# Query and key transposes of two batches moved from TensorE to the DMA crossbar, in a kernel of windowed attention and a SwiGLU block

## The chip, the cores and the metric

The kernel runs on one core of one Trainium2 chip. The metric is the device time of one execution in microseconds (us). The kernel before was run three times: 268.59, 268.65 and 269.51 us, median 268.65. A profiled execution is longer than its span (first to last instruction) by what lies around it.

## The reference

Attention over 4 batches of 8 heads, 768 positions and 64 elements a head, in which a query sees the 8 first keys ("global") and the 96 last ones up to its own ("local"), with a bias that falls with the distance by a slope of its head; its result, 3072 tokens of 512 elements, goes through a SwiGLU block with 1536 inner elements.

```python
scores = scale * np.matmul(q, k.transpose(0, 1, 3, 2))
is_global = pos[None, :] < n_global
is_local = (rel >= 0) & (rel < n_local)            # rel = query - key
scores = np.where(is_global | is_local, scores + bias, -1e9)
a = softmax(scores)                                # over the keys
x = np.matmul(a, v)  ->  [B * S, H * D]
g = x @ w_gate
out = (g * sigmoid(g) * (x @ w_val)) @ w_out
```

Inputs and output are fp32; the kernel computes in fp16 with fp32 sums.

## The kernel before

**Attention.** The unit of work is a pair of heads (`Pair(b, hp)`, four pairs in each batch), as two heads of 64 elements fill 128 partitions. Keys are cut into 7 chunks of 120, and each chunk is stored as 128 columns of `kT`, the 8 global keys first (columns 0 to 7), then its 120 own. So a query window of 216 meets its global and its local keys in one matmul. `transposes` (L186) makes `qT` and `kT` of a pair: 24 TensorE transposes of 128x64 blocks (L193) from the staged rows `qst` and `kst` into PSUM, then ScalarE copies them out: `qT` (L198) and `kT` in two pieces (L204, on VectorE for batch 0), then a VectorE copy spreads the 8 global keys over the 7 chunks (L208). `qst` and `kst` have two buffers each; their rows hold 6 positions of a head side by side, so that each piece of a load is 768 bytes in SBUF. `scores` (L212) multiplies a third of the chunks ("bank" 0, 1 or 2), takes the exponential on ScalarE (L227) and multiplies with the mask on VectorE or GpSimd (L234 for bank 1, L238 for the others). `values` (L240) sums denominators (`den`) and numerators (`num`) for half of the positions; VectorE inverts (L269, L270) and spreads (L275) the denominators, ScalarE copies `num` to `ns` (L290), and GpSimd multiplies into `xT` (L279).

**Feed-forward.** Tokens go in 8 blocks `t` of 384, two to a batch. For each block and each of 12 slices `f` of 128 inner elements there is a group of 4 gate matmuls and one of 4 value matmuls (L307), a tanh on ScalarE (L318), two VectorE products (L320, L324), and from block 1 on a quarter of an output tile of the block before, 3 matmuls (L334). Gate and value products share three PSUM banks. Every fourth quarter completes an output tile, which ScalarE copies to `osb` (two buffers, L339) and SyncE stores (L341).

**What sets the order.** The order of each engine's work is written out by hand. The loop at the end goes through the feed-forward groups; each group earns a share `work * quota` of an attention step, and each time a whole step is owed the next one in `plan` is emitted. `plan` gives each run of blocks a list of steps: `first(b)` has transposes, scores and values of the first half of batch `b`, `second(b)` the second half, and `both(b)` mixes the second half of batch `b` with the first half of `b + 1`: 13 steps, over blocks 2 and 3 for batch 2 and blocks 4 and 5 for batch 3, though a list starts as soon as the one before is used up.

Loads are issued by GpSimd (they cast fp32 to fp16), through the table `loads`, whose index is 12 `t` + `f`:

```python
    def both(b):
        x, y = second(b), first(b + 1)
        return x[:3] + [y[0], x[3]] + y[1:]
...
    for b, base, step in ((2, 15, 1), (3, 32, 2)):
        loads[base] = [lambda b=b: (stage(b), load_qk(b, 0, 4))]
        loads[base + step] = [lambda b=b: load_qk(b, 4, 8)]
        for c in range(NCH):
            loads[base + step * (2 + c)] = [lambda b=b, c=c: load_v_rest(b, c)]
```

SyncE's queue carries, after the start, the output stores alone. GpSimd's carries loads, mask products and `xT` products in one order.

Of the kernel before, what the change touches and what calls it, by code (L numbers as in the profile page):

```python
# [10 lines left out]
FP16 = mybir.dt.float16  # L11
# [4 lines left out]
KC = 120  # L16
# [21 lines left out]
def kernel(  # L38
# [12 lines left out]
    nc = tc.nc  # L51

    B, H, S, D = q.shape
    NG, NL = int(n_global), int(n_local)
    assert (B, H, S, D) == (4, 8, 768, 64)
    assert (NG, NL) == (8, 96)
    NP = H // 2
# [6 lines left out]
    NCH = 7  # L64
# [16 lines left out]
    sb = ctx.enter_context(tc.tile_pool(name="sb", bufs=1))  # L81
    sb2 = ctx.enter_context(tc.tile_pool(name="sb2", bufs=2))
    sb3 = ctx.enter_context(tc.tile_pool(name="sb3", bufs=3))
    ps = ctx.enter_context(tc.tile_pool(name="ps", bufs=1, space=bass.MemoryType.PSUM))

    ctx.enter_context(tc.manual_schedule())
# [10 lines left out]
    kTs = [sb.tile([128, NCH * 128], FP16, name=f"kT{i}") for i in range(NP)]  # L97
# [8 lines left out]
    def stage(b):  # L106
        qst[b] = sb2.tile([128, H, J * D], FP16, name="qst", tag="qst")
        kst[b] = sb2.tile([128, H, J * D], FP16, name="kst", tag="kst")

    def load_qk(b, h0, h1):  # L110
        for st, src in ((qst[b], q), (kst[b], k)):
            nc.gpsimd.dma_start(  # L112
                out=st[:, h0:h1, :],
                in_=src[b, h0:h1].rearrange("h (p j) d -> p h (j d)", p=128))
# [6 lines left out]
    def load_v_rest(b, c):  # L121
        n = min(KC, S - KC * c)
        nc.gpsimd.dma_start(  # L123
            out=vSs[b][NG:NG + n, c, :, :],
            in_=v[b, :, KC * c:KC * c + n, :].rearrange("h p d -> p h d"))
# [4 lines left out]
    def load_globals():  # L130
        nc.gpsimd.dma_start(
            out=vG.rearrange("p b h d -> p (b h) d"),
            in_=v[:, :, 0:NG, :].rearrange("b h p d -> p (b h) d"))
        for b in range(B):
            nc.sync.dma_start(
                out=vSs[b][0:NG, :, :, :],
                in_=vG[:, b, :, :].unsqueeze(1).broadcast_to([NG, NCH, H, D]))

    wg = sb.tile([128, NC, DFF], FP16, name="wg")
    wv = sb.tile([128, NC, DFF], FP16, name="wv")  # L140
# [22 lines left out]
    def bank(name, dt=FP32, cols=512):  # L163
        tags = state["tags"]
        tag = tags[state["n"] % len(tags)]
        state["n"] += 1
        return ps.tile([128, cols], dt, name=name, tag=tag)
# [13 lines left out]
    class Pair:  # L181
# [4 lines left out]
        def transposes(self):  # L186
            b, hp = self.b, self.hp
            trq = bank("trq", FP16, S)
            trk = bank("trk", FP16, S)
            for st, tr in ((qst[b], trq), (kst[b], trk)):  # L190
                for j in range(J):
                    for hi in range(2):
                        nc.tensor.transpose(  # L193
                            tr[64 * hi:64 * hi + 64, 128 * j:128 * j + 128],
                            st[:, 2 * hp + hi, D * j:D * j + D], ident)
            self.qT = sb2.tile([128, S], FP16, name="qT", tag="qT", bufs=NP)
            self.kT = kTs[hp]
            nc.scalar.copy(  # L198
                out=self.qT.rearrange("r (p j) -> r p j", j=J),
                in_=trq.rearrange("r (j p) -> r p j", j=J))  # L200
            k3 = self.kT.rearrange("r (c m) -> r c m", m=128)
            t3 = trk.rearrange("r (j p) -> r p j", j=J)
            for c0, c1, n in ((0, 6, KC), (6, 7, S - 6 * KC)):
                (nc.vector.tensor_copy if b == 0 else nc.scalar.copy)(  # L204
                    out=k3[:, c0:c1, NG:NG + n].rearrange("r c (p j) -> r c p j", j=J),
                    in_=t3[:, 20 * c0:20 * c0 + (c1 - c0) * (n // J), :].rearrange(
                        "r (c p) j -> r c p j", c=c1 - c0))
            nc.vector.tensor_copy(  # L208
                out=k3[:, :, 0:NG],
                in_=k3[:, 0, NG:2 * NG].unsqueeze(1).broadcast_to([128, NCH, NG]))  # L210

        def scores(self, bk, mul_eng):  # L212
            hp = self.hp
            sc = [bank("scA"), bank("scB")]
            for c in range(NCH):
                cb, col, q0, n = chunks[c]
                if cb != bk:
                    continue
                for hi in range(2):
                    r = slice(64 * hi, 64 * hi + 64)  # L220
                    nc.tensor.matmul(  # L221
                        sc[hi][:, col:col + n],
                        lhsT=self.kT[r, 128 * c:128 * c + 128],
                        rhs=self.qT[r, q0:q0 + n], start=True, stop=True)
            for hi in range(2):
                at = sb2.tile([128, BANK], FP16, name="at", tag=f"at{hi}{bk}", bufs=NP)
                nc.scalar.activation(out=at, in_=sc[hi][:, 0:BANK], func=AF.Exp, scale=scale)  # L227
                self.at[hi, bk] = at
            for hi in range(2):
                at = self.at[hi, bk]  # L230
                m = masks[:, 2 * hp + hi, :]
                if bk == 1:
                    a2 = at.rearrange("p (c w) -> p c w", c=2)
                    mul_eng.tensor_mul(  # L234
                        a2, a2, m[:, WIN:2 * WIN].unsqueeze(1).broadcast_to([128, 2, WIN]))
                else:
                    o = WIN // 2 * bk
                    mul_eng.tensor_mul(at, at, m[:, o:o + BANK])  # L238
# [111 lines left out]
    stage(1)  # L350
    load_qk(0, 0, 2)
    load_globals()
    load_v(0, 0)
    load_v(0, 1)
# [16 lines left out]
    pairs = {(b, hp): Pair(b, hp) for b in range(B) for hp in range(NP)}  # L371
# [15 lines left out]
    for t in range(4 + 2 * (NP - 1)):  # L387
# [3 lines left out]
        for hp in range(NP):  # L391
            s = t - 2 * hp
# [17 lines left out]
    def sc(b, hp, bk):  # L410
        on_vector = b == 0 or bk == 0 or (bk == 2 and hp % 2 == 0)
        return lambda: pairs[b, hp].scores(bk, nc.vector if on_vector else nc.gpsimd)

    def va(b, hp, half):
        return lambda: pairs[b, hp].values(half, b == 0)

    def tr(b, hp):
        return pairs[b, hp].transposes

    def second(b):  # L420
        return [[sc(b, 0, 2), sc(b, 1, 2)], [sc(b, 2, 2), sc(b, 3, 2)],
                [va(b, 0, 1), va(b, 1, 1)], [va(b, 2, 1), va(b, 3, 1)]]

    def first(b):
        return [[tr(b, 0), tr(b, 1)],
                [sc(b, 0, 0), sc(b, 0, 1)], [sc(b, 1, 0), sc(b, 1, 1)],
                [va(b, 0, 0), tr(b, 2)], [sc(b, 2, 0), sc(b, 2, 1)],
                [va(b, 1, 0), tr(b, 3)], [sc(b, 3, 0), sc(b, 3, 1)],
                [va(b, 2, 0)], [va(b, 3, 0)]]

    def both(b):
        x, y = second(b), first(b + 1)
        return x[:3] + [y[0], x[3]] + y[1:]


    single = [[sc(0, 0, 2)], [sc(0, 1, 2)], [va(0, 0, 1)], [sc(0, 2, 2)],
              [va(0, 1, 1)], [tr(1, 0)], [sc(0, 3, 2)], [va(0, 2, 1)], [va(0, 3, 1)], [tr(1, 1)]]
    plan = [((0,), single), ((1,), first(1)[1:]), ((2, 3), both(1)),
            ((4, 5), both(2)), ((6,), second(3))]

    loads = {10: [lambda: load_qk(1, 4, 8)]}
    for c in range(4, NCH):
        loads[8 + c] = [lambda c=c: load_v_rest(1, c)]
    for b, base, step in ((2, 15, 1), (3, 32, 2)):
        loads[base] = [lambda b=b: (stage(b), load_qk(b, 0, 4))]
        loads[base + step] = [lambda b=b: load_qk(b, 4, 8)]
        for c in range(NCH):
            loads[base + step * (2 + c)] = [lambda b=b, c=c: load_v_rest(b, c)]


    NT = TOK // TB
# [79 lines left out]
```

The softmax here doesn't subtract the row's maximum and nothing guards it: scores larger than these inputs give would overflow.

## Time and profile before

| what | value |
|---|---|
| median of three runs | 268.65 us |
| the profiled execution: its time | 268.58 us |
| the profiled execution: its span | 266.7 us |
| mean granted TensorE clock | 0.986 |
| 192 + 192 transposes on TensorE, mean of one | 239 and 243 ns |
| copies of `qT` on ScalarE, 16 | 12.9 us busy |
| copies of `kT` on ScalarE, 12 + 12 | 9.3 + 2.8 us busy |
| loads of `qst` and `kst` of batches 2 and 3 | 384 KB each, four to a batch |
| output stores on SyncE | 24, 256 KB, 2.0 us to landing |

In the profile a line such as `L193` is a line of the kernel, PE is TensorE, DVE VectorE, ACT ScalarE, POOL GpSimd and SP SyncE; `trq<-ident,qst` says what an instruction writes and reads. A row of 40 digits gives the busy share of an engine in tenths for 40 equal slices of the span. The chain is followed back from the last instruction, at each step to what released it. In a timeline, each row has a start, a length and, in brackets, the idle time before it with its releaser; the DMA-issuing instructions of GpSimd appear as `DMA_DIRECT2D`. Tokens of block 1 are under way on TensorE from about 54 to 86 us, those of block 2 to about 118, of block 3 to about 149.

### The profile page before, as it was taken

What the parts mean: (1) busy time and instruction counts of PE and PEld (TensorE: products, weight loads), DVE (VectorE), ACT (ScalarE), POOL (GpSimd) and SP (SyncE); (2) the same over time, 40 slices, a digit from 0 to 9 for tenths busy, and PEclk for the clock granted to TensorE, in tenths of its full rate; (3) what the DMA queues carried; (4) which work ended last, traced back from release to release, by engine and by line L of the source; (5) the groups of instructions that cost most, each with busy time, mean ns of one, the idle gap of its engine ahead of it and who ended that gap; (6) DMA issues with size and microseconds to landing.
All of it is one profiled execution on the core that took longest, in us unless ns stands there. A gap on an engine that the chain in (4) does not pass through costs nothing.

```text
span 266.7 us, 5704 instructions
## 1 busy us (share of the span) xinstructions
PE 247.8 (93%) x2240; PEld 142.0 (53%) x2240; DVE 174.8 (66%) x389; ACT 140.9 (53%) x297; POOL 112.1 (42%) x130
## 2 busy tenths in 40 slices
PE   1668899899999999999999999999999999999993
PEld 0444456456556555555556555565566555555541
DVE  2488799786877576557767485766778655555610
ACT  3657745678466656755464656573572333332321
POOL 8985562268987226365565152414342200000000
PEclk9995999999999999999999999999999999999999
DMA  8999999955996100967545200100110111001122
GB/s 103 168 167 195 193 205 206 177 57 34 209 176 42 47 39 2 157 91 101 65 60 37 49 19 24 39 28 15 42 39 2 39 42 41 21 18 42 39 79 79
DMA packets 45529, 21.27 MB, mean 80 GB/s; under 512 B 28256, under 2 KB 42432, under 8 KB 45504
## 3 DMA queue, kind: packets, MB, share of 16 engines
q0 software_dynamic: 41504, 14.20, 46.8%
q1 hardware_dynamic: 4000, 6.72, 6.9%
q8 instruction: 17, 0.28, 0.4%
q14 instruction: 8, 0.07, 0.1%
HBM read 28.58 MB, written 6.29 MB: 131 GB/s over the span
## 4 chain that ended last, share of the span: by engine, by line
PE 74%; DMA 12%; POOL 5%; ACT 5%; issue 2%; DVE 1%; ACTq 0%; POOLq 0%
PE ops L334 23%; PE vps L307 21%; PE gps L307 19%; DMA kst<-in_k_dram 8%; DMA wv<-in_moe_w_val_dram 4%; PE den L256 3%; PE num L256 3%; PE scA L221 3%; ACT at L227 2%; POOL vS L117 1%; PE trq L193 1%; POOL qst L112 1%; PE trk L193 1%; ACT kT L204 1%; ACT osb L339 1%
## 5 line engine op out<-in xcount | busy, mean ns | idle before, releaser
L318 ACT ACTIVATE th<-gps 128x384 f32<-128x384 f32 x96 | 47.9, 499 | 65.2 <-PE gps L307 64.2
L320 DVE SCALAR_TENSOR_TENSOR sl<-th,gps 128x384 f32<-128x384 f32 x96 | 52.6, 548 | 42.9 <-ACT th L318 42.3
L307 PE MATMUL gps<-xT,wg 128*128 128x384 f16 x384 | 79.1, 327 | 0.8 <-DVE xT L282 0.5
L307 PE MATMUL vps<-xT,wv 128*128 128x384 f16 x384 | 79.1, 327 | 0.7 <-DVE sl L320 0.7
L334 PE MATMUL ops<-wo,hT 128*128 128x512 f16 x288 | 76.0, 379 | 0.6 <-ACT osb L339 0.6
L324 DVE TENSOR_TENSOR hT<-vps,sl 128x384 f16<-128x384 f32 x96 | 52.7, 549 | 8.7 <-PE vps L307 1.1
L307 PEld LDWEIGHTS <-wg 128*128 128x128 f16 x384 | 36.1, 98 | 32.9 <-issue 1.9
L307 PEld LDWEIGHTS <-wv 128*128 128x128 f16 x384 | 36.2, 98 | 26.9 <-issue 4.0
L279 POOL TENSOR_TENSOR xT<-ns,rb 128x384 f16<-128x384 f32 x24 | 23.9, 997 | 59.4 <-DVE rb L275 52.3
L334 PEld LDWEIGHTS <-hT 128*128 128x128 f16 x288 | 27.1, 98 | 25.4 <-issue 1.2
L227 ACT ACTIVATE at<-scA 128x432 f16<-128x432 f32 x48 | 25.8, 537 | 16.6 <-PE scB L221 16.6
L234 POOL TENSOR_TENSOR at<-at,masks 128x432 f16<-128x432 f16 x24 | 23.7, 1010 | 15.7 <-ACT at L227 10.3
L227 ACT ACTIVATE at<-scB 128x432 f16<-128x432 f32 x48 | 26.1, 543 | 0.0
L339 ACT ACTIVATE osb<-ops 128x512 f32<-128x512 f32 x24 | 14.4, 602 | 18.7 <-PE ops L334 18.5
L123 POOL DMA_DIRECT2D vS<-in_v_dram x24 | 21.6, 901 | 3.9 <-DMA wo<-in_moe_w_out_dram 1.6
L238 DVE TENSOR_TENSOR at<-at,masks 128x432 f16<-128x432 f16 x52 | 20.4, 413 | 3.8 <-ACT at L227 3.3
L256 PE MATMUL den<-at,ones 128*64 128x216 f16 (+6 forms) x288 | 17.8, 238 | 1.8 <-DVE at L234 1.3
L290 ACT COPY ns<-num 128x384 f32<-128x384 f32 x24 | 11.5, 478 | 14.3 <-PE num L256 12.1
L275 DVE STREAM_TRANSPOSE rb<-dR 128x384 f32<-128x384 f32 x32 | 18.3, 572 | 1.0
L269 DVE STREAM_TRANSPOSE dT<-den 128x384 f32<-128x384 f32 x32 | 18.2, 569 | 0.3 <-PE den L256 0.3
L256 PEld LDWEIGHTS <-ones 128*64 128x64 f16 x288 | 11.9, 113 | 11.8 <-issue 10.6
L221 PE MATMUL scA<-qT,kT 64*128 64x216 f16 (+2 forms) x112 | 14.9, 255 | 3.0 <-DVE kT L208 2.9
(32 smaller groups left out, 182.0 us busy)
## 6 DMA issues: line engine op xcount, KB each, us to landing
out_dram<-osb SPq DMA_DIRECT2D x24, 256.0 KB, 2.0
vS<-in_v_dram POOLq DMA_DIRECT2D x20, 120.0 KB, 4.5
qst<-in_q_dram POOLq DMA_DIRECT2D x5, 384.0 KB, 5.6
kst<-in_k_dram POOLq DMA_DIRECT2D x5, 384.0 KB, 7.8
wg<-in_moe_w_gate_dram POOLq DMA_DIRECT2D x4, 384.0 KB, 8.8
wv<-in_moe_w_val_dram POOLq DMA_DIRECT2D x4, 384.0 KB, 10.0
wo<-in_moe_w_out_dram POOLq DMA_DIRECT2D x3, 512.0 KB, 14.0
qst<-in_q_dram POOLq DMA_DIRECT2D x6, 192.0 KB, 6.0
```

What stands on the lines that cost most here:

```text
L123: nc.gpsimd.dma_start(out=vSs[b][NG:NG + n, c, :, :], in_=v[b, :, KC * c:KC * c + n, :].rearrange("h p d -> p h d"))
L221: nc.tensor.matmul(sc[hi][:, col:col + n], lhsT=self.kT[r, 128 * c:128 * c + 128], rhs=self.qT[r, q0:q0 + n], start=True, stop=True)
L227: nc.scalar.activation(out=at, in_=sc[hi][:, 0:BANK], func=AF.Exp, scale=scale)
L234: mul_eng.tensor_mul(a2, a2, m[:, WIN:2 * WIN].unsqueeze(1).broadcast_to([128, 2, WIN]))
L238: mul_eng.tensor_mul(at, at, m[:, o:o + BANK])
L256: nc.tensor.matmul(dst[r, o:o + n], lhsT=ones if ones_side else vSs[b][:, c, 2 * hp + hi, :], rhs=self.at[hi, cb][:, col:col + n], start=( ...
L279: nc.gpsimd.tensor_mul(dst, ns[:, 0:n_q], rb[:, 0:n_q])
L307: nc.tensor.matmul(gv[f, which][:, 0:TB], lhsT=w[:, c, 128 * f:128 * f + 128], rhs=xT[:, c, TB * t:TB * t + TB], start=(c == 0), stop=(c = ...
L318: nc.scalar.activation(out=th, in_=dst[:, 0:TB], func=AF.Tanh, scale=0.5)
L320: nc.vector.scalar_tensor_tensor(out=sl, in0=th, scalar=1.0, in1=dst[:, 0:TB], op0=AluOp.add, op1=AluOp.mult)
L324: nc.vector.tensor_mul(hTs[t][:, f, :], dst[:, 0:TB], gv["sl"])
L334: nc.tensor.matmul(ops, lhsT=hTs[t][:, f, 128 * i:128 * i + 128], rhs=wo[:, f, :], start=(f == 0), stop=(f == NFF - 1))
```

## The change

For batches 2 and 3 `transposes` and the loads of `qst` and `kst` are no longer used. `cast_qk` has GpSimd copy four heads of q or k from DRAM to DRAM with the cast to fp16, into a scratch tensor of 768 rows of 512 elements (all heads of a position side by side). Then SyncE issues one crossbar transpose for q and one for k of each pair: 768 rows x 128 columns of the scratch to 128 partitions x 768. `qT` is complete with that. For keys the result goes to a new tile `kN` (four buffers), and `spread_keys` copies it into the chunks of `kT` with three VectorE copies. `both` becomes a list of 11 steps written out, with the issue of the crossbar transposes (`fetch`) in the first two steps and the spreading (`sp`) in the fourth and the sixth. The casts take the places of the loads: k ahead of q, for batch 2 two at index 15 and two at 16, for batch 3 one at each of 32 to 35; the value loads keep their indices.

```diff
+    def cast_qk(b, i, h0, h1):
+        nc.gpsimd.dma_start(
+            out=qk_dr[b, i].rearrange("s (h d) -> h s d", d=D)[h0:h1],
+            in_=(q, k)[i][b, h0:h1])
...
+        def transposes_dma(self):
+            b, hp = self.b, self.hp
+            self.qT = sb2.tile([128, S], FP16, name="qT", tag="qT", bufs=NP)
+            self.kN = sb2.tile([128, S], FP16, name="kN", tag="kN", bufs=NP)
+            f = slice(128 * hp, 128 * hp + 128)
+            nc.sync.dma_start_transpose(out=self.kN, in_=qk_dr[b, 1][:, f])
+            nc.sync.dma_start_transpose(out=self.qT, in_=qk_dr[b, 0][:, f])
+
+        def spread_keys(self):
+            self.kT = kTs[self.hp]
+            k3 = self.kT.rearrange("r (c m) -> r c m", m=128)
+            n = KC * (NCH - 1)
+            nc.vector.tensor_copy(
+                out=k3[:, 0:NCH - 1, NG:],
+                in_=self.kN[:, 0:n].rearrange("r (c m) -> r c m", m=KC))
+            nc.vector.tensor_copy(out=k3[:, NCH - 1, NG:NG + S - n], in_=self.kN[:, n:S])
+            nc.vector.tensor_copy(
+                out=k3[:, :, 0:NG],
+                in_=self.kN[:, 0:NG].unsqueeze(1).broadcast_to([128, NCH, NG]))
...
     def both(b):
-        x, y = second(b), first(b + 1)
-        return x[:3] + [y[0], x[3]] + y[1:]
+        n = b + 1
...
+        return [[sc(b, 0, 2), sc(b, 1, 2), fetch(0, 1)], [sc(b, 2, 2), sc(b, 3, 2), fetch(2, 3)],
+                [va(b, 0, 1), va(b, 1, 1)], [va(b, 2, 1), va(b, 3, 1), sp(0, 1)],
+                [sc(n, 0, 0), sc(n, 0, 1)], [sc(n, 1, 0), sc(n, 1, 1), sp(2, 3)],
+                [va(n, 0, 0), sc(n, 2, 0)], [sc(n, 2, 1), va(n, 1, 0)],
+                [sc(n, 3, 0), sc(n, 3, 1)], [va(n, 2, 0)], [va(n, 3, 0)]]
...
     for b, base, step in ((2, 15, 1), (3, 32, 2)):
-        loads[base] = [lambda b=b: (stage(b), load_qk(b, 0, 4))]
-        loads[base + step] = [lambda b=b: load_qk(b, 4, 8)]
+        for i in range(2):
+            for h in range(2):
+                loads.setdefault(base + step * (h + 2 * i) // 2, []).append(
+                    lambda b=b, i=i, h=h: cast_qk(b, 1 - i, 4 * h, 4 * h + 4))
```

More of the change, by code (lines that the diff above doesn't have):

```diff
@@ L83 @@
     sb3 = ctx.enter_context(tc.tile_pool(name="sb3", bufs=3))
+    dram = ctx.enter_context(tc.tile_pool(name="dram", bufs=1, space=bass.MemoryType.DRAM))
     ps = ctx.enter_context(tc.tile_pool(name="ps", bufs=1, space=bass.MemoryType.PSUM))
@@ L137, in load_globals @@
                 in_=vG[:, b, :, :].unsqueeze(1).broadcast_to([NG, NCH, H, D]))
+    by_dma = (2, 3)
+    qk_dr = {(b, i): dram.tile([S, H * D], FP16, name=f"dr{i}{b}")
+             for b in by_dma for i in range(2)}
+    def cast_qk(b, i, h0, h1):
+        nc.gpsimd.dma_start(
+            out=qk_dr[b, i].rearrange("s (h d) -> h s d", d=D)[h0:h1],
+            in_=(q, k)[i][b, h0:h1])
     wg = sb.tile([128, NC, DFF], FP16, name="wg")
@@ L431, in both, with fetch, sp @@
     def both(b):
-        x, y = second(b), first(b + 1)
-        return x[:3] + [y[0], x[3]] + y[1:]
+        n = b + 1
+        def fetch(*hps):
+            return lambda: [pairs[n, hp].transposes_dma() for hp in hps]
+        def sp(*hps):
+            return lambda: [pairs[n, hp].spread_keys() for hp in hps]
+        return [[sc(b, 0, 2), sc(b, 1, 2), fetch(0, 1)], [sc(b, 2, 2), sc(b, 3, 2), fetch(2, 3)],
[3 more added lines that the diff above has]
+                [sc(n, 3, 0), sc(n, 3, 1)], [va(n, 2, 0)], [va(n, 3, 0)]]
     single = [[sc(0, 0, 2)], [sc(0, 1, 2)], [va(0, 0, 1)], [sc(0, 2, 2)],
@@ L444 @@
     for b, base, step in ((2, 15, 1), (3, 32, 2)):
-        loads[base] = [lambda b=b: (stage(b), load_qk(b, 0, 4))]
-        loads[base + step] = [lambda b=b: load_qk(b, 4, 8)]
+        for i in range(2):
+            for h in range(2):
+                loads.setdefault(base + step * (h + 2 * i) // 2, []).append(
+                    lambda b=b, i=i, h=h: cast_qk(b, 1 - i, 4 * h, 4 * h + 4))
         for c in range(NCH):
-            loads[base + step * (2 + c)] = [lambda b=b, c=c: load_v_rest(b, c)]
+            loads.setdefault(base + step * (2 + c), []).append(
+                lambda b=b, c=c: load_v_rest(b, c))
     NT = TOK // TB
```

## The prediction

> **What bounds the kernel now.** I read the page's busy shares and its 40 slices first, then the chain of work that ended last, then the waits of TensorE, and at last the timelines of TensorE, GpSimd and SyncE around the steps that the change touches.
>
> The page:
> ```profile
> PE 247.8 (93%) x2240; PEld 142.0 (53%) x2240; DVE 174.8 (66%) x389; ACT 140.9 (53%) x297; POOL 112.1 (42%) x130
> PE   1668899899999999999999999999999999999993
> ...
> PE 74%; DMA 12%; POOL 5%; ACT 5%; issue 2%; DVE 1%; ACTq 0%; POOLq 0%
> ```
> From about 50 us to the end TensorE is never under nine tenths, and the chain is mostly its matmuls. DMA and GpSimd stand in the chain for the first 50 us, which this change leaves alone. So from 50 us on an instruction taken out of TensorE's stream is worth its full time, if no other engine then stops the stream. TensorE's waits there are few; two follow the work that is removed:
> ```profile
> 87.73 0.53 PE L193 MATMUL trq<-ident,qst 128*64 128x128 f16 x12
> 88.09 0.50 PE L193 MATMUL trk<-ident,kst 128*64 128x128 f16 x12
> 88.42 0.50 PE L193 MATMUL trq<-ident,qst 128*64 128x128 f16 x12
> 88.76 0.50 PE L193 MATMUL trk<-ident,kst 128*64 128x128 f16 x12
> 89.19 0.82 PE L307 MATMUL gps<-xT,wg 128*128 128x384 f16 x4
> ...
> 92.37 0.81 PE L307 MATMUL vps<-xT,wv 128*128 128x384 f16 x4 [0.40 <-DVE sl L320]
> ...
> 149.52 0.81 PE L334 MATMUL ops<-wo,hT 128*128 128x512 f16 x3 [0.57 <-ACT osb L339]
> ```
> Columns: start, length, what, and in brackets the idle time before it. Lengths of pipelined matmuls overlap; starts tell the cost: two pairs of heads cost 89.19 - 87.73 = 1.46 us.
>
> [...] all casting loads are on POOL's queue. So the new path needs two transfers in series on two queues. [...] Pieces of 128 B into SBUF ran at about 150 GB/s in this trace (the value loads at 75 to 77 us), 768 B ones at 205; writes of them into DRAM aren't shown.
>
> **The change, part by part** (one profiled execution: span 266.7 us, its own time 268.58; the median of the runs is 268.65, so I sum against 268.58).
>
> 1. TensorE, removed: 192 of the 384 transposes, eight pairs. In each batch one group of two pairs (1.46 us by the starts, at 87.73 and 145.37) and two single pairs behind value matmuls (106.70 to 107.47 and so on, 0.77 us each): 1.46 + 2 x 0.77 = 3.00, twice is 6.0 us. The two double groups also interrupt the feed-forward stream for themselves (ops start at 86.99, three matmuls take 0.65, the group starts at 0.74): 0.1 each, 0.2. All on the path.
>
> 2. ScalarE, removed: 8 x (0.81 qT + 0.78 and 0.23 kT) = 14.6 us of copies, all off the path but for the two waits above, 0.40 + 0.57 = 0.97 us, which come as its copies hold back the tanh and osb. Gain 1.0. Sum so far **-7.2**. Next late after these: TensorE itself, no other engine.
>
> 3. GpSimd, added. The same number of issues (4 per batch), but 3072 pieces each (four heads x 768 rows) where a load had 512. Issue times in the trace: 512 pieces 0.78 us, 960 pieces 0.97, so 0.42 ns a piece; 3072 give 0.97 + 2112 x 0.00042 = 1.86, 1.08 us more each. Batch 2's are at 64 to 70 us, where GpSimd is full:
> ```profile
> 64.34 0.79 POOL L112 DMA_DIRECT2D qst<-in_q_dram  x1
> 65.12 0.77 POOL L112 DMA_DIRECT2D kst<-in_k_dram  x1
> 67.32 0.99 POOL L279 TENSOR_TENSOR xT<-ns,rb 128x384 f16<-128x384 f32 x1 [1.43 <-DVE rb L275]
> 68.27 0.81 POOL L112 DMA_DIRECT2D qst<-in_q_dram  x1
> 69.07 0.76 POOL L112 DMA_DIRECT2D kst<-in_k_dram  x1
> 69.82 1.99 POOL L234 TENSOR_TENSOR at<-at,masks 128x432 f16<-128x432 f16 x2
> ```
> Adding 4.3 us and using up the 1.43 of idle moves the mask products from 69.82 to 72.8, done 74.8. Their reader, the values of pair 3, is on TensorE at 73.94: **+0.9**. Bounds: nothing (if issue time doesn't grow with pieces) to 2. The xT product behind it moves from 76.7 to 79.6, but its first reader is block 2 at 85.69: free. Batch 3's casts, at 106 to 117 us, meet idle gaps of 1 to 3 us and are free. Also, each GpSimd issue waits for the landing of the one eight before it (seen at 23 to 47 us: "POOL qst L112 <- DMA wv" and the like). v loads 4 to 6 of batch 2 then wait for casts; behind them are mask and xT products. This bites only if the casts land after about 82 to 85 us.
>
> 4. VectorE, added: the two spreading copies and the 128x56 one, for two pairs at a time, in four bursts. The 128x720 copy from PSUM took 902 ns, the upper end; [...] The small ones are 0.20 and 0.18 to 0.24. [...] The bursts of 3.4 us that ScalarE had at 88.3 and 145.9 cost TensorE 0.40 and 0.57; VectorE has a third of its time idle. I take 0.2 each, **+0.8**; bounds 0 and 2.4. TensorE's cover is the three PSUM banks for gate and value products, about 1.5 us ahead; without it the whole burst is paid.
>
> 5. SyncE, added: 16 crossbar transposes of 768x128 fp16 (196.6 KB), no such row in the trace. [...] A gain is excluded, as nothing on SyncE is taken away. [...] Queued behind them on SyncE are only the output stores, one about each 10 us with two osb buffers, so some 15 us of delay are free.
>
> 6. The waits. The first transposes sit behind the scores that stand at 76.65 us, and wait for the casts. With 4 engines a cast is 768 pieces per engine at 13.3 ns (128 B x 16 / 154 GB/s) = 10.2 us plus about 2 to land; issued until 66.2, 68.1, 70.9 and 72.8 they land at 78.5, 80.4, 83.2 and 85.1. SyncE issues in order k0, q0, k1, q1, so k of pair 1 sits behind q of pair 0: 85.1 + 2 x 2.4 + 2 = 91.9. VectorE comes to its spread one step after the values at 83, about 88.5 us, and waits 3.4; behind it on VectorE are sl and hT of the feed-forward, for which TensorE waits after its 1.5 us of lead: **+2.0**. The second spread of batch 2 (about 101.5) needs k of pair 3, six transposes after 85.1: 101.5, just in time. Batch 3's casts are done by some 130, its transposes start at about 132, and its spreads are 15 and 25 us later: free.
>
> Bounds of step 6: nothing, if the casts use all engines (2.6 us each, the last landing at 77.4); +12.2 if DRAM writes of 128 B cost twice as much (+10.2).
>
> Sum: 268.58 - 7.2 + 0.9 + 0.8 + 2.0 = **265.1 us**.
>
> **The rivals.** (a) *All is hidden*: casts on all engines, step 6 falls away: 263.1, or 261.4 without steps 3 and 4 too. For it: the slack of 12 us between fetch and spread. [...] (b) *No change to be measured*: GpSimd's and VectorE's costs at their upper ends, 2 + 2.4 + 2.0 = 6.4 of the 7.2 are eaten: 267.8. Against: VectorE's idle third. (c) *Casts twice as slow*: 265.1 + 10.2 = 275.3[...]. (d) *Slower: the crossbar itself.* With T us for each transpose, the spreads of pairs 2 and 3 wait 6T - 15.9 us in batch 2 (landing 87.1 + 6T against 101.5 + 1.5) and 7T - 24.5 in batch 3. Against 5.5 us that steps 1 to 4 leave, it decides from T = 3.6 us on; at 4.5 it is 268.58 - 5.5 + 11.1 + 7.0 = 281[...]. [...] That VectorE waits at the spread would show it.
>
> **How the numbers follow.** 265.1: 0.30; (a) 0.24; (b) 0.12; (c) 0.14; (d) 0.20. A difference of 0.5% (1.3 us) is about what a measurement of this kernel can tell from none. Faster by more: the forecast and (a), 0.54; same: nearly all of (b), 0.11; slower: (c), (d) and a little of (b), 0.35. The range goes from 261.0 (steps 3, 4 and 6 at nothing) to 284, which takes in (c) and (d) up to T of 4.7 us and leaves about 0.15 out, nearly all above. The faster cases alone lie in 261 to 267.
>
> **What would show it.** Right: TensorE has 192 fewer transposes, ScalarE is about 14.6 us less busy, GpSimd's cast issues are near 1.9 us each, TensorE waits near 74 and near 90 us for a VectorE that itself waits for a crossbar DMA of batch 2, and none like it in batch 3. Cast landings of 12 us confirm the 4 engines, 5 us rival (a), over 20 rival (c). Transposes of over 3.6 us each, with waits in batch 3 too, are rival (d). Wrong: a new wait elsewhere, such as ScalarE's osb waiting for stores behind the transposes, or GpSimd stopped by the eight-back rule past 85 us.

## The result, and the profile after

The changed kernel takes **363.1 us** (median of 4 runs, 363.05 to 365.3) against 268.84 us of the kernel before (4 runs, 268.59 to 269.51): 1.352 times as long, 95% interval 1.346 to 1.358. The forecast was 265.1 us, and the range ended at 284. Now and then an execution has a lower granted clock and takes longer (412.11 us at a clock of 0.583 for the first kernel with positions outermost, 325.75 us at 0.771 for the kernel before); such executions are left out of every time and ratio below.

The page of the changed kernel, the rows that answer to those shown of before:
```profile
span 361.2 us, 5341 instructions
...
PE 251.8 (70%) x2048; PEld 140.8 (39%) x2048; DVE 182.6 (51%) x405; ACT 129.2 (36%) x273; POOL 136.4 (38%) x130
...
PE   1779989840000756989425005999999999999995
...
PE 41%; issue 27%; POOL 15%; DMA 9%; DVE 4%; ACT 2%; POOLq 0%; ACTq 0%; DVEq 0%
```
TensorE has its 192 instructions fewer and ScalarE is 11.7 us less busy, as the change is meant to do. But TensorE's row has holes, slices 9 to 14 (72 to 126 us) and 20 to 24 (172 to 217 us). In the chain, TensorE's share fell from 74% to 41%, and "issue", time in which an engine waits for nothing that the profile shows, is 27%.

Who waits for whom in the changed kernel, TensorE first (us in total, times, longest):
```profile
PE den L287 <- POOL at L265: 81.6, 6, 42.9
PE trq L204 <- DMA qst<-in_q_dram: 6.8, 2, 6.0
PE den L287 <- POOL at L269: 6.5, 2, 5.9
```
and GpSimd:
```profile
POOL dr L146 <- issue: 72.8, 6, 13.2
```
TensorE waits 81.6 + 6.5 = 88.1 us for mask products of GpSimd, nearly the whole loss of 94.5 us in span. GpSimd, in turn, stands still for 72.8 us ahead of six of its eight casts (L146), and no instruction releases it. There is no wait of VectorE for `kN`: the crossbar and the spread are not in this.

The timeline of GpSimd in the changed kernel, the casts of batch 2:
```profile
64.71 3.81 POOL L146 DMA_DIRECT2D dr<-in_k_dram  x1
81.49 3.75 POOL L146 DMA_DIRECT2D dr<-in_k_dram  x1 [12.97 <-issue]
85.25 1.00 POOL L310 TENSOR_TENSOR xT<-ns,rb 128x384 f16<-128x384 f32 x1
97.82 3.79 POOL L146 DMA_DIRECT2D dr<-in_q_dram  x1 [11.56 <-issue]
...
114.01 3.76 POOL L146 DMA_DIRECT2D dr<-in_q_dram  x1 [12.40 <-issue]
117.79 1.96 POOL L265 TENSOR_TENSOR at<-at,masks 128x432 f16<-128x432 f16 x2
```
A cast is 3.8 us of issuing, then GpSimd stands still for 11.6 to 13 us before the next one. The mask product for pair 3 of batch 1, which stood at 69.82 us before, runs at 117.79. TensorE's values wait behind it:
```profile
118.85 0.28 PE L287 MATMUL den<-at,ones 128*64 128x144 f16 x1 [42.89 <-POOL at L265]
```

The DMA part of the page says what a cast has become:
```profile
q0 software_dynamic: 135712, 14.49, 53.8%
...
dr<-in_k_dram POOLq DMA_DIRECT2D x4, 384.0 KB, 16.3
dr<-in_q_dram POOLq DMA_DIRECT2D x4, 384.0 KB, 17.6
...
kN<-dr SPq DMA_TRANSPOSE x8, 6.7
qT<-dr SPq DMA_TRANSPOSE x8, 9.1
```
Columns of the first row: packets, MB, share of 16 engines' time; of the others: count, size, us to landing. GpSimd's queue had 41504 packets and 14.20 MB before. Take off the 8 loads of 512 pieces that went, and the 8 casts hold 135712 - 37408 = 98304 packets, **12288 each**. The pieces of 128 bytes are 3072 (four heads x 768 rows); the other 9216 are packets of 4 bytes: the packet records of this queue hold 76576 of that size, against 2848 before, 73728 more. 3072 is 4 x 768 and 9216 is 12 x 768. I read that as 768 pieces on each of four of the sixteen engines and as many 4-byte entries on each of the twelve others; the records do not name the engine of a packet. And each of the first three casts of batch 2 lands some 16 us after its issue starts, at 81.08, 97.50 and 113.70 in the trace; the next issue starts 0.3 to 0.4 us after that, at 81.49, 97.82 and 114.01.

### The profile page after: what moved, and what is told of

Read it like the earlier page. It is cut to its first block, busy times and chain, and to the rows that moved or that the text cites. A ratio compares the mean times of both kernels' runs of the same rounds, so it can differ in the third digit from the quotient of the medians.

```text
span 361.2 us, 5341 instructions
## 1 busy us (share of the span) xinstructions
PE 251.8 (70%) x2048; PEld 140.8 (39%) x2048; DVE 182.6 (51%) x405; ACT 129.2 (36%) x273; POOL 136.4 (38%) x130
## 3 DMA queue, kind: packets, MB, share of 16 engines
q0 software_dynamic: 135712, 14.49, 53.8%
q1 hardware_dynamic: 16800, 9.87, 12.2%
## 4 chain that ended last, share of the span: by engine, by line
PE 41%; issue 27%; POOL 15%; DMA 9%; DVE 4%; ACT 2%; POOLq 0%; ACTq 0%; DVEq 0%
PE ops L365 13%; PE vps L338 12%; PE gps L338 11%; POOL dr L146 6%; DMA kst<-in_k_dram 4%; DMA wv<-in_moe_w_val_dram 3%; POOL at L265 2%; DMA vS<-in_v_dram 2%; POOL vS L124 2%; PE den L287 2%; PE num L287 2%; POOL xT L310 2%; PE scA L252 1%; ACT at L258 1%; POOL vS L118 1%
## 5 line engine op out<-in xcount | busy, mean ns | idle before, releaser
L287 PE MATMUL den<-at,ones 128*64 128x216 f16 (+6 forms) x288 | 19.8, 240 | 90.5 <-POOL at L265 81.6
L338 PE MATMUL gps<-xT,wg 128*128 128x384 f16 x384 | 80.7, 333 | 1.9 <-DVE hT L355 0.9
L338 PE MATMUL vps<-xT,wv 128*128 128x384 f16 x384 | 81.2, 334 | 0.8 <-DVE sl L351 0.6
L365 PE MATMUL ops<-wo,hT 128*128 128x512 f16 x288 | 78.6, 390 | 0.3
L300 DVE STREAM_TRANSPOSE dT<-den 128x384 f32<-128x384 f32 x32 | 20.4, 638 | 81.3 <-PE den L287 81.3
L355 DVE TENSOR_TENSOR hT<-vps,sl 128x384 f16<-128x384 f32 x96 | 52.7, 549 | 16.3 <-PE vps L338 9.0
L287 PEld LDWEIGHTS <-ones 128*64 128x64 f16 x288 | 12.7, 113 | 101.1 <-issue 99.5
L338 PEld LDWEIGHTS <-wg 128*128 128x128 f16 x384 | 37.0, 99 | 35.7 <-issue 5.3
L321 ACT COPY ns<-num 128x384 f32<-128x384 f32 x24 | 11.5, 481 | 103.8 <-PE num L287 89.2
L146 POOL DMA_DIRECT2D dr<-in_q_dram x4 | 15.1, 3774 | 46.6 <-issue 46.6
L124 POOL DMA_DIRECT2D vS<-in_v_dram x24 | 21.7, 905 | 18.9 <-issue 12.4
L146 POOL DMA_DIRECT2D dr<-in_k_dram x4 | 15.1, 3784 | 26.2 <-issue 26.2
## 6 DMA issues: line engine op xcount, KB each, us to landing
wv<-in_moe_w_val_dram POOLq DMA_DIRECT2D x4, 384.0 KB, 10.2
dr<-in_k_dram POOLq DMA_DIRECT2D x4, 384.0 KB, 16.3
```

The source lines that it names most:

```text
L124: nc.gpsimd.dma_start(out=vSs[b][NG:NG + n, c, :, :], in_=v[b, :, KC * c:KC * c + n, :].rearrange("h p d -> p h d"))
L146: nc.gpsimd.dma_start(out=qk_dr[b, i].rearrange("s (h d) -> h s d", d=D)[h0:h1], in_=(q, k)[i][b, h0:h1])
L287: nc.tensor.matmul(dst[r, o:o + n], lhsT=ones if ones_side else vSs[b][:, c, 2 * hp + hi, :], rhs=self.at[hi, cb][:, col:col + n], start=( ...
L300: nc.vector.transpose(dT[:, 0:n_q], den[:, 0:n_q])
L338: nc.tensor.matmul(gv[f, which][:, 0:TB], lhsT=w[:, c, 128 * f:128 * f + 128], rhs=xT[:, c, TB * t:TB * t + TB], start=(c == 0), stop=(c = ...
L355: nc.vector.tensor_mul(hTs[t][:, f, :], dst[:, 0:TB], gv["sl"])
```

## The experiments

**Theory A**, drawn from this profile: with the heads as slowest dimension the pieces of a cast go to 4 engines (3072 = 4 x 768), and the 9216 packets of 4 bytes make it 768 entries on every one of 16; beside so many a second cast finds no room, so GpSimd holds until the first has landed (81.08, next issue at 81.49), and the mask products behind it are late. **Rival B**: writing 128-byte pieces to DRAM is slow in itself. **Rival C**: the crossbar transposes, the spread or the new order of steps cost most.

### Positions outermost, same bytes and pieces

```diff
-            out=qk_dr[b, i].rearrange("s (h d) -> h s d", d=D)[h0:h1],
-            in_=(q, k)[i][b, h0:h1])
+            out=qk_dr[b, i].rearrange("s (h d) -> s h d", d=D)[:, h0:h1],
+            in_=(q, k)[i][b, h0:h1].rearrange("h s d -> s h d"))
```


> The changed kernel with one edit: the four-head cast names the 768 positions ahead of the 4 heads on both sides, the same bytes and the same 3072 pieces. Theory A[...]: 192 pieces on each of 16 engines, so about 3072 packets in place of 12288, an issue of about 1.9 us, landings of 5 to 7 us, no idle on GpSimd ahead of a cast, and a total of 261 to 267 us. Rival B (writing 128-byte pieces to DRAM is slow in itself, some 16 us for each cast however it is spread): landings stay near 16 us and the total stays over 330. Rival C (the crossbar transposes and the spread cost most): casts get fast, but the total stays over 275.

Measured: 265.8 us (3 runs), ratio 0.989 (0.981 to 0.998). The same kernel once more, for a narrower interval and a profile:

> The changed kernel with the positions outermost in the casts, once more, for a tighter interval and a profile at full clock. Theory A with the steps of the prediction: 6.0 us of TensorE transposes are gone, GpSimd's four casts of batch 2 cost 4 x 1.25 us more than the loads did (2.03 against 0.78) in a stretch where GpSimd is full, so TensorE waits some 2 to 3 us for a mask product of batch 1, and the spread bursts cost under 1 us: 265 to 266.5 us, ratio about 0.988. If the spreads wait for the crossbar after all, waits of VectorE on kN would show and explain the missing gain in place of GpSimd.

Measured: **266.0 us** (6 runs, 265.55 to 266.37), ratio 0.9895 (0.987 to 0.992). Its page:
```profile
q0 software_dynamic: 61984, 14.20, 57.7%
...
dr<-in_k_dram POOLq DMA_DIRECT2D x4, 384.0 KB, 8.0
dr<-in_q_dram POOLq DMA_DIRECT2D x4, 384.0 KB, 7.8
```
61984 is 37408 + 8 x 3072 to the packet: the 9216 packets of 4 bytes a cast are gone. Landings halve (8 us; 5 to 7 were expected), an issue takes 2.03 us in place of 3.78, and GpSimd stands still ahead of no cast. B falls, as the pieces and their size are the same, and C falls, as the crossbar path, the spread and the order of steps are all still there. One part of what was expected did not come: TensorE hardly waits for a mask product of GpSimd (2 to 3 us were expected). It waits for VectorE's `sl`:
```profile
PE vps L338 <- DVE sl L351: 2.5, 4, 0.9
PE den L287 <- POOL at L265: 0.2, 1, 0.2
```

### The casts alone, on top of the kernel before

Two kernels with the loads, TensorE transposes and steps of before, and the eight casts added at their places, their results unused: once as in the change, once with the positions outermost.
```diff
+        for i in range(2):
+            for h in range(2):
+                loads.setdefault(base + step * (h + 2 * i) // 2, []).append(
+                    lambda b=b, i=i, h=h: cast_qk(b, 1 - i, 4 * h, 4 * h + 4))
```


> The kernel before, with its loads and TensorE transposes kept, and the eight casts of the changed kernel added at the same places of GpSimd's order, their result unused. Theory A: the eight casts hold GpSimd for some 12 us each as they do in the changed kernel, so nearly the whole loss comes back without any crossbar transpose: 345 to 375 us. Rival C: most of the loss is in the transposes, the spread or the new order of steps: under 310 us.

Measured: 369.0 us (one run). The casts by themselves cost 100 us, all of the loss and a little more. This agrees with A.

> The kernel before with the eight casts added, their result unused, in the form with the positions outermost. This is the price of the casts by themselves in that form. Theory A: 8 x 1.9 us more on GpSimd and no holds, part of it hidden: 269 to 274 us. Rival B: over 340.

Measured: 275.7 us, ratio 1.025 (1.016 to 1.034), above the 269 to 274 expected. Where it comes from is seen in the timeline of GpSimd:
```profile
65.16 4.05 POOL L145 DMA_DIRECT2D dr<-in_k_dram  x2
69.19 1.04 POOL L289 TENSOR_TENSOR xT<-ns,rb 128x384 f16<-128x384 f32 x1
70.14 0.81 POOL L113 DMA_DIRECT2D qst<-in_q_dram  x1
70.95 0.77 POOL L113 DMA_DIRECT2D kst<-in_k_dram  x1
71.68 4.04 POOL L145 DMA_DIRECT2D dr<-in_q_dram  x2
75.71 1.99 POOL L244 TENSOR_TENSOR at<-at,masks 128x432 f16<-128x432 f16 x2
```
8.1 us of issues with no gap between them: the mask product is at 75.71 in place of 69.82. In the profiled execution (273.9 us, the fastest of the four) the output tile that ScalarE copies at 85.89 us before comes at 91.12, 5.2 us late, after batch 2's casts; the one at 247.16 comes at 252.81, 5.65 us late. So batch 3's casts, in a stretch where GpSimd has gaps, cost 0.4. That much of the prediction's step 3, full in batch 2 and free in batch 3, held.

### Quarter casts, still four heads

```diff
-        nc.gpsimd.dma_start(
-            out=qk_dr[b, i].rearrange("s (h d) -> h s d", d=D)[h0:h1],
-            in_=(q, k)[i][b, h0:h1])
+        for s0 in range(0, S, S // 4):
+            s = slice(s0, s0 + S // 4)
+            nc.gpsimd.dma_start(
+                out=qk_dr[b, i].rearrange("s (h d) -> h s d", d=D)[h0:h1, s],
+                in_=(q, k)[i][b, h0:h1, s])
```


> The changed kernel with each cast cut into four of 192 positions, still 4 heads as the slowest dimension, so still 4 engines, with a quarter of the entries each. Theory A: [...] GpSimd's holds shrink, though 16 issues in place of 4 come under the rule that an issue waits for the one eight before it: 275 to 320 us. If successive casts go to the same four engines, or if the write itself is slow (B), the drain stays 16 us for four quarters and the total stays at 350 to 370.

Measured: 314.3 us (one run). GpSimd's timeline, columns as above:
```profile
64.41 6.82 POOL L148 DMA_DIRECT2D dr<-in_k_dram  x5
72.07 1.36 POOL L148 DMA_DIRECT2D dr<-in_k_dram  x1 [0.84 <-issue]
73.98 1.36 POOL L148 DMA_DIRECT2D dr<-in_k_dram  x1 [0.55 <-issue]
77.10 1.36 POOL L148 DMA_DIRECT2D dr<-in_k_dram  x1 [1.76 <-issue]
```
The 32 quarter casts have 136096 - 37408 = 98688 packets, 3084 each, so about 192 for each of sixteen engines. Five of them, 5 x 192 = 960 entries an engine by this count, go out back to back; the sixth, which would make 1152, waits and starts at 72.07, 0.33 us after the first has landed (71.74), the seventh 0.31 us after the second, and so on. The holds are shorter, 19.6 us in 18 of them, and the casts overlap: the sixteen quarters of batch 2 are issued within 34 us, where four whole casts took 53 us. This agrees with A, and it says how much was let out in these two traces: 960 entries for each engine and not 1152 here, with the next issue 0.31 to 0.33 us behind a landing. In the changed kernel the count fits behind the last cast of batch 2: three value loads of 960 pieces, 60 for each of sixteen engines, pass, 768 + 180 = 948, and the fourth, which would make 1008, waits 11.2 us and starts at 134.69, after that cast has landed (134.38). The number of transfers is not what counts: one is enough to hold the next in the changed kernel, and it takes five here.

### Eight heads

```diff
-            for h in range(2):
-                loads.setdefault(base + step * (h + 2 * i) // 2, []).append(
-                    lambda b=b, i=i, h=h: cast_qk(b, 1 - i, 4 * h, 4 * h + 4))
+            loads.setdefault(base + step * i, []).append(
+                lambda b=b, i=i: cast_qk(b, 1 - i, 0, 8))
```


> The changed kernel with each pair of four-head casts made one of eight heads, the heads still the slowest dimension, now 8: two casts to a batch. Theory A: 8 engines with 768 pieces each and 8 with as many 4-byte entries, so the queue is full after each cast as before, a cast takes about the same 16 us with twice the data, packets on the casting queue fall by half of the surplus (to about 86000), and there is one hold between two casts of a batch in place of three: 295 to 320 us. If it is the number of 128-byte writes that costs the time (rival B), two casts of twice the size take 32 us each and the total stays at 350 to 370.

Measured: 297.9 us (one run). Page and timeline of GpSimd:
```profile
q0 software_dynamic: 86496, 14.30, 57.1%
...
dr<-in_k_dram POOLq DMA_DIRECT2D x2, 768.0 KB, 16.7
dr<-in_q_dram POOLq DMA_DIRECT2D x2, 768.0 KB, 19.2
```
```profile
64.40 3.77 POOL L146 DMA_DIRECT2D dr<-in_k_dram  x1
...
81.44 3.79 POOL L146 DMA_DIRECT2D dr<-in_q_dram  x1 [10.94 <-issue]
```
Twice the data land in nearly the same 17 us with the same 3.8 us of issue, and the packets of a cast are as many: (86496 - 37408) / 4 = 12272, about 768 for each of sixteen engines. Two casts are held, for 21.3 us, in place of six for 72.8, and 29 us of the loss are left. The packets in the traces show the rate: while casts alone move, 309 pieces start in a microsecond with four heads (72 to 79 us), 618 with eight (71 to 78 us) and 1226 with the positions outermost (71 to 78 us). With 4, 8 and 16 engines that is 13 ns a piece on each, an estimate, as the engines are counted from the packets. Rival B is out by this too: the same 128-byte pieces start at four times the rate when only their order differs.

### Batch 3 alone

The form with positions outermost, with `by_dma = (3,)` and the old loads and steps for batch 2.

> The kernel with the positions outermost, but only batch 3 by way of the crossbar; batch 2 keeps its loads, its TensorE transposes and its old steps. If GpSimd's fullness at 64 to 75 us eats batch 2's part of the gain, this one keeps batch 3's 3.0 us and more and is as fast as the one with both, 264.5 to 266. If each batch gains alike, half of the gain is left: 266.5 to 267.5 us.

Measured: 268.5 us (20 runs), ratio 0.9994 (0.998 to 1.001), so no gain at all, and neither of the two expectations. TensorE waits 1.24 us at 152.4 and 0.58 at 162.4 for VectorE's `sl` after the spread bursts, and 0.52 at 121.7; the rest of the 3 us removed is not in a wait that I can name. How the gain divides between the batches stays open.

### Few pieces for GpSimd: contiguous casts, laid out by SyncE

GpSimd casts q or k of a whole batch to a contiguous fp16 copy, and SyncE copies that inside DRAM into rows of 512:
```diff
+    def cast_qk(b, i):
+        nc.gpsimd.dma_start(
+            out=qk_flat[b, i].rearrange("h (p j) d -> (h p) (j d)", p=16),
+            in_=(q, k)[i][b].rearrange("h (p j) d -> (h p) (j d)", p=16))
+
+    def lay_out(b, i):
+        nc.sync.dma_start(
+            out=qk_dr[b, i].rearrange("s (h d) -> s h d", d=D),
+            in_=qk_flat[b, i].rearrange("h s d -> s h d"))
...
```


> GpSimd casts q or k of a whole batch contiguously (128 rows of 3072 elements on both sides, so few and long pieces, one issue of some 0.7 us in place of two of 2.03), and SyncE copies the fp16 result inside DRAM into rows of 512 elements, positions outermost, before the crossbar transposes it. Theory A says that the pieces of a casting transfer are what GpSimd pays for: its issues fall from 8 us to 1.4 in batch 2, the mask product of pair 3 is no later than before, VectorE's mask products are no longer held up while GpSimd issues, and the total is 262 to 264.5 us. Against it: if two more transfers in series on SyncE make the transposes late, VectorE's spread waits for them and the total stays at 266 or above.

Measured: 272.4 us (6 runs), ratio 1.0145 (1.011 to 1.018): 1.5% slower. The GpSimd part came out as expected: an issue is 0.55 us and the mask product of pair 3 is at 69.35. But VectorE now waits for the crossbar, which was never so in the changed kernel:
```profile
DVE kT L243 <- DMA kN<-dr: 6.3, 2, 4.4
```
and TensorE with it, in its timeline:
```profile
97.49 1.44 PE L346 MATMUL vps<-xT,wv 128*128 128x384 f16 x4 [5.53 <-DVE sl L359]
```
Three transfers in series (cast 7 to 9 us to landing, copy 12 to 14, transposes 4) are too long for that place.

> The same with the largest of the three spreading copies (128x720) on ScalarE in place of VectorE. If VectorE's bursts are what still costs, another 0.5 to 1.5 us are saved; if TensorE's tanh wait on ScalarE is as near, the time is the same within 0.5 us of the run beside it, or longer.

```diff
-            nc.vector.tensor_copy(
+            nc.scalar.copy(
                 out=k3[:, 0:NCH - 1, NG:],
```
Measured: 272.1 us (6 runs), ratio 1.012 (1.009 to 1.015), within 0.5 us of the run beside it. The same wait of 5.8 us hides what the copy would show; nothing follows on VectorE's bursts.

Then both casts three slices earlier, the copies at the next two, and k of two pairs ahead of their q (against the kernel with contiguous casts):
```diff
...
-            return lambda: [pairs[n, hp].transposes_dma() for hp in hps]
+            return lambda: ([pairs[n, hp].transposes_dma() for hp in hps],
+                            [pairs[n, hp].transposes_q() for hp in hps])
...
-            loads.setdefault(base + step * i, []).append(
+            loads.setdefault(base - 3 + i, []).append(
                 lambda b=b, i=i: cast_qk(b, 1 - i))
-            loads.setdefault(base + step * (2 + i), []).append(
+            loads.setdefault(base - 1 + i, []).append(
                 lambda b=b, i=i: lay_out(b, 1 - i))
```


> The contiguous cast with both casts of a batch issued three slices earlier (indices 12 and 13 for batch 2), the copies inside DRAM at the two next, and the k transposes of two pairs ahead of their q ones. In the run before it, VectorE waited 6.3 us for kN in batch 2 and TensorE 5.5 us for VectorE. If that chain of transfers in series was the whole of what stood against the gain, it is ready some 6 us sooner, the wait goes, and the total is 262 to 265 us, faster than the kernel before and than the form with positions outermost (0.9895 of before). If the copy on SyncE, some 5 us for each issue with the output stores behind it, costs by itself, ScalarE will wait for osb and the total stays at 267 or above.

Measured: **263.9 us** (6 runs, 263.32 to 265.58), ratio 0.983 (0.980 to 0.987): 1.7% faster than the kernel before. By the medians it is also faster than the form with positions outermost, though the two intervals touch. VectorE waits 0.2 us for `kN`, and TensorE and ScalarE don't wait for a free `osb`. The page:
```profile
PE 241.6 (92%) x2048; PEld 136.9 (52%) x2048; DVE 179.9 (69%) x405; ACT 129.1 (49%) x273; POOL 108.3 (41%) x126
```
TensorE is 6.2 us less busy than before, the span 5.4 us shorter. The idea of the change is worth what the prediction's steps 1 and 2 said, less about 2 us, once GpSimd doesn't pay for it. Two waits of TensorE behind bursts of VectorE's spread make up 1.5 of these 2 us:
```profile
102.87 0.81 PE L350 MATMUL gps<-xT,wg 128*128 128x384 f16 x4 [0.94 <-DVE hT L367]
157.45 0.81 PE L350 MATMUL vps<-xT,wv 128*128 128x384 f16 x4 [0.58 <-DVE sl L363]
```

## Why the prediction was wrong

**The step that failed is step 3**, with the part of step 6 that relied on it. Step 3 let GpSimd go on as soon as a cast was issued, and so put at nothing the wait of one cast for the one before it; the runs showed 72.8 us of it, and through the mask products behind it 88.1 us of TensorE's waits. I looked at the wait for the transfer eight before, which the trace of before showed (eleven waits of 0.27 to 1.77 us, from 15.97 to 46.72), and not at how much may be under way at once. No wait for room is named in that trace. The price of an issue was wrong too, which is the smaller part. Step 3 took "3072 pieces each" and a slope of 0.42 ns a piece for 1.86 us an issue. With the four engines that step 6 assumed, the entries are four times as many: 12288 packets, 3.78 us. The count was what I had wrong: 3072 pieces on sixteen engines took 2.03 us, near the forecast, and the 9216 entries of 4 bytes another 1.75, 0.19 ns each. This makes four issues of 3.8 us, some 12 us more in batch 2.

**Step 6**: the four engines, which no trace of before showed, fit the packet counts (4 x 768 and 12 x 768); right were also the 13.3 ns a piece (13 by the estimate from 309 pieces in a microsecond) and the 12.2 us from the end of an issue to landing: 12.1 to 12.6 for the first three casts of batch 2. The 16.3 us of the page are counted from the start of the issue. But the casts were to overlap, issued until 72.8; they ran one after another, the last issued from 114.0 on. The stall was put at VectorE's spread; it fell on TensorE's values by way of GpSimd's mask products, from 75.96 us on, 12 us before the first spread was due. The list of signs had a stop of GpSimd as its last item, but past 85 us and by the eight-back rule, and gave it neither a price nor a rival. That rule is not what held the casts: each issue started 0.3 to 0.4 us after the cast just before it had landed.

**Step 1** was right: 6.2 us less of TensorE in the last experiment. **Step 2**: 11.7 us less of ScalarE in place of 14.6, as copies one behind the other overlap in the busy time (in the kernel before, the two pieces of a `kT` take 0.87 us together at 88.99); its two waits are gone in the last version. **Step 4**: the 128x720 copy takes 0.33 to 0.34 us when undisturbed, against the 0.90 from PSUM in the kernel before that step 4 took as its upper end; nothing in the trace of before showed a lower one. A burst takes 0.9 us by itself and 2.5 where GpSimd multiplies masks beside it (91.55 and 102.24 with positions outermost), and the price was 0.8 where the last version shows the 1.5 above. **Step 5** was too high: SyncE issues transposes 1.3 us apart in the last experiments, with 3.6 to 4.4 us to landing, against the 2.4 each that step 6 counts with, an estimate of mine that rests on no run: the trace of before has no such row. Rival (d), the crossbar, is out: VectorE waits 0.2 us for `kN` in the last version. Rival (c), twice as slow a cast, is out with the 13 ns a piece; that 128-byte writes to DRAM are slower was not shown.

The form with positions outermost is what rival (a) described, casts on all engines: 263.1 was its price, 266.0 was measured. What TensorE waits for there is VectorE: 3.7 us in all for `sl` and `hT`, against 1.0 in the kernel before. With positions outermost, two mask products of VectorE during the casts take
```profile
68.31 2.99 DVE L269 TENSOR_TENSOR at<-at,masks 128x432 f16<-128x432 f16 x2
```
where the same two took 0.81 us before, and TensorE waits 0.80 us for `sl` at 71.8. A second wait for `sl`, 0.95 us at 86.4, follows two mask products of VectorE that took 4.08 us from 81.79, while GpSimd multiplied masks. How much of the missing 3 us these are was not separated. Why VectorE takes longer while GpSimd issues was not shown. With the contiguous casts the mean of these products is 405 ns again, against 541 here.

**Accounted for**: span less busy time of TensorE went from 18.9 to 109.4 us, 90.5 more, of which 88.1 are its waits for mask products of GpSimd. Its busy time went from 247.8 to 251.8, 4.0 more, although 6.2 us of transposes are gone: the same 2048 instructions take 241.6 in the last experiment, so 10.2 us are, by my estimate, the slow matmuls after the stalls, where the granted clock was 0.50 for 21.1 us in all (below). 90.5 + 4.0 are the 94.5.

## What to carry to other kernels

In these runs a casting DMA was paid on GpSimd by packets, not by bytes: the same 384 KB took 3.78 us of issue with 12288 packets and 2.03 us with 3072, and 768 KB took 3.8 us with 12272. Put a long dimension, as the 768 positions here, outermost on both sides, look at the packet count of its queue before anything else, and compare it with the number of pieces: a surplus, as the 9216 packets of 4 bytes a cast here, is paid too. Before a large transfer is put into an in-order queue that also carries compute, ask whether what is already under way leaves room for it, and name what stands behind it. A transfer off the critical path cost 94 us here, as a small product that TensorE needs was queued after it.

## What the runs showed that was not expected

- GpSimd went on issuing up to 960 entries for each engine (quarter casts) and not up to 1008 (the fourth value load behind a cast). These are estimates: packets by sixteen engines, over the transfers that had not landed. All 38 issues that would have gone to 1008 or more, in the four kernels with four or eight heads outermost, were held, and each started 0.31 to 0.42 us after a landing. A four-head cast has 3072 packets of 128 bytes and 9216 of 4, and none of the 9216 with the positions outermost.
- After four stalls of the changed kernel TensorE worked at half rate for a while: the granted clock was still 0.50 for 5.4, 3.7, 5.5 and 6.5 us after stalls of 42.9, 5.9, 11.5 and 25.2 us. After the first, groups of four matmuls start 1.28 us apart until 124.4 us and 0.65 apart from then on:
```profile
PEclk9999999995555696999958555999999999999999
...
121.82 1.49 PE L338 MATMUL gps<-xT,wg 128*128 128x384 f16 x4
123.10 1.39 PE L338 MATMUL vps<-xT,wv 128*128 128x384 f16 x4
...
125.56 0.81 PE L338 MATMUL gps<-xT,wg 128*128 128x384 f16 x4
126.21 0.81 PE L338 MATMUL vps<-xT,wv 128*128 128x384 f16 x4
```
- A VectorE copy of 48 or 56 columns, 0.17 us by itself, takes 0.97 to 1.00 us when a mask product of GpSimd runs at the same time. While GpSimd issued the first cast of the changed kernel, until 68.52, a copy of 56 columns took 2.79 us from 65.71 and ended with it; before, it took 0.18.
